# Norm powers by square root, reciprocal and a Newton step in lots; a planner that books the port of POOL and DVE; earlier first weight loads

## The chip, the cores and the metric

The kernel runs on one core of one Trainium2 chip. The metric is the device time of one execution in microseconds (us); the kernel before has a median of 950.0 us in 3 runs (944.38 to 951.93). The engines are TensorE (PE in the profile, its weight loads PEld), VectorE (DVE), ScalarE (ACT), GpSimd (POOL) and SyncE (SP), which issues every DMA here.

## The reference, cut to what matters

Three stages follow each other, all in float32. Attention without a softmax: B=4 batches, H=8 heads, S=576 rows, D=64:

```
kv  = einsum('bhsd,bhse->bhde', k, v)
out = einsum('bhsd,bhde->bhse', q, kv)
x   = out / sqrt(mean(out*out, -1) + 1e-6) * g_norm      # (4,8,576,64)
x   = x.transpose(0,2,1,3).reshape(2304, 512)
x   = (x @ w_a) * (x @ w_b) @ w_out                      # first MoE, d_ff 1536
x   = sigmoid(x @ w_gate) * (x @ w_val) @ w_out2         # second MoE
```

## The kernel before

**Attention.** The 2304 tokens are 18 tiles of 128 (`NTILE`). For each batch b, `keys_values` loads four blocks of keys and values (640 KB each), PE multiplies them into bank `o1` (L388) and ACT and DVE copy the result into `kvbd` (L399, L402). For each tile t, `queries` loads q (256 KB), PE multiplies (`O`, L422), ACT squares (L431), DVE sums the squares of each head (`ss`, L435), POOL scales (L439) and takes the power -0.5 of 128x8 elements (`rr`, L441), DVE multiplies PSUM by it (`xn`, L445), PE transposes (`T`, L452) and ACT writes the tile of x into `part` (`Y`, L458). Tiles 0 to 11 hold their product in one of the banks `u0` to `u5`; tiles 12 to 17 hold theirs in `o0` or `o1`, which the down products use too.

**Weights.** Each of 24 blocks F of 128 columns has tiles a, b and o (512 KB each, 64-bit numbers). `weights` loads one into a ring of two `raw` buffers (L208). ACT (L217, L221), DVE (L225, L227, L231) and POOL (L237) round it to float32 by integer operations. `w_parts` forms sums of the quarters on DVE (L256, L257, L262, L263) and splits each part into a high half on ACT (L273) and a low half (L277).

**MoE.** A group is a stage m, a pair of blocks q and one of three token ranges j; there are 36, in the order m, q, j. Each matrix product takes seven products of quarters (`SLOTS`, `ORDER`), 6 matmuls of 128x384 each (L494), for two blocks u and v; eight down products of the group before stand between them (`down`, L586, evicted at L594, L596, L598). With q = 0, `x_comb` builds the seven inputs of a range: DVE sums (`xs`, L307), ACT high halves (L326), low halves (`xl`, L329), and a store; later groups load them again.

**Order.** Nothing is ordered by hand. Every piece of work is an `op` with an engine, a planned duration, its predecessors, the buffers that it takes, and a due time. `Plan.order` runs the dues back from the products (the first is due at 38,000 ns) and then runs an event simulation: whenever an engine is free it takes the ready op with the earliest due time for which the buffer rings have room. What the plan does in turn is the program order of each engine, the SP queue of DMAs included; on the chip each engine keeps to that order. Ops with the two engines `LO` (the low halves, L277, L329, L566) go to whichever of DVE and POOL takes them first; DVE, which the loop over engines reaches before POOL, is planned at 0.55 of POOL's duration.

Of the kernel before, what the change touches and what calls it, by code (L numbers as in the profile page):

```python
# [23 lines left out]
P = 128  # L24
# [3 lines left out]
N = 384  # L28
# [21 lines left out]
ANY_ORDER = ("o0", "o1")  # L50


class Plan:


# [1 line left out]
    def __init__(self):  # L57
        self.ops, self.by, self.n = [], {}, 0

    def op(self, name, eng, ns, fn, after=(), new=(), uses=(), due=None, lag=150):  # L60
        o = dict(name=name, eng=(eng,) if isinstance(eng, str) else eng, ns=ns, fn=fn, new=list(new),
                 uses=list(uses) + [b for _, b in new], due=due, lag=lag, succ=[], need=0, at=None)
        self.by[name] = o
        o["after"] = list(after)
        self.ops.append(o)

    def order(self):
# [26 lines left out]
        events = [(0, i, "ready", o) for i, o in enumerate(ops) if not o["need"]]  # L94
        heapq.heapify(events)
        count, done = len(ops), []

        def room(o):
            for tag, b in o["new"]:
# [7 lines left out]
        while events:  # L107
            t = events[0][0]
            while events and events[0][0] <= t:
                _, _, what, o = heapq.heappop(events)  # L110
                if what == "ready":
                    for e in o["eng"]:
                        ready[e].append(o)
                elif what == "done":
                    for b in o["uses"]:
                        users[b] -= 1
                elif what == "lag":
                    for s in o["succ"]:
                        s["need"] -= 1
                        if not s["need"]:  # L120
                            for e in s["eng"]:
                                ready[e].append(s)
            for e in free_at:
                if free_at[e] > t:
                    continue
                best = None
                for o in ready[e]:
                    if (best is None or o["due"] < best["due"]) and room(o):
                        best = o
                if best is None:  # L130
                    continue
                for x in best["eng"]:
                    ready[x].remove(best)
                for tag, b in best["new"]:
                    ring = rings[tag]
                    if len(ring) >= RINGS.get(tag, 1):
                        ring.pop(0)
                    ring.append(b)
                    nxt[tag] += 1
                ns = best["ns"] * (0.55 if len(best["eng"]) == 2 and e == "DVE" else 1)  # L140
                best["at"], best["on"] = t, e
                done.append(best)
                free_at[e] = t + ns
                for end, what in ((t + ns, "done"), (t + ns, "free"), (t + ns + best["lag"], "lag")):
                    count += 1
                    heapq.heappush(events, (end, count, what, best))
# [6 lines left out]
def attention_then_two_moes(  # L153
# [22 lines left out]

    ident = one.tile([P, P], F32, name="ident")
    gcol = one.tile([P, 1], F32, name="gcol")
    mhalf = one.tile([P, H], F32, name="mhalf")
    kvbd = [one.tile([P, KC, P], F32, name=f"kvbd{i}") for i in range(2)]  # L180

    part = [one.tile([P, 2, KC, N], F32, name=f"part{j}") for j in range(NJ)]
# [9 lines left out]
        return 160 + 1.04 * n  # L192

    def pool(n):
        return 230 + 2.2 * n

    def dma(kb):
        return 150 + kb * 1024 / 390

    LO = ("POOL", "DVE")  # L200


    def weights(F, which):
        k = (F, which)
# [34 lines left out]
            )  # L239

        raw, m, l, w = (("raw", k), ("mag", k), ("last", k), ("w32", k))
        op(("load", k), "SP", dma(512), load, new=[("raw", raw)], lag=2000)
        op(m, "ACT", 670, mag, [("load", k)], [("mag", m)], [raw])
        op(l, "ACT", 670, last, [("load", k)], [("last", l)], [raw])
        op(("clamp", k), "DVE", 900, clamp, [m], uses=[m])
        op(("sign", k), "DVE", 750, sign, [("clamp", k)], uses=[raw, m])
        op(w, "POOL", 1400, rounded, [("sign", k), l], [("w32", w)], [m, l])

    def w_parts(F):

# [11 lines left out]
            V.tensor_tensor(out=t[:, 0:256], in0=tl[b][:, 256:512], in1=t1[:, 0:256], op=ALU.subtract)  # L262
            V.tensor_tensor(out=t[:, 256:512], in0=tl[a][:, 256:512], in1=t[:, 0:256], op=ALU.subtract)  # L263

        op(t13, "DVE", 950, sums13, [a, b], [("tmp", t13)], [a, b])
        op(t24, "DVE", 950, sums24, [t13], [("tmp", t24)], [a, b, t13])

        def parts(i, src, cut, n):
            name = ("wo" if i == "o" else f"wp{i}", F)

            def hi():
                tl[name] = new_tile(name[0], [2, n], F32R)
                A.activation(out=tl[name][:, 0, :], in_=tl[src][:, cut], func=ACTF.Copy)  # L273

            def lo(eng):
                t = tl[name]
                eng.tensor_tensor(out=t[:, 1, :], in0=tl[src][:, cut], in1=t[:, 0, :], op=ALU.subtract)  # L277

            op((*name, "h"), "ACT", act(n), hi, [src], [(name[0], name)], [src])
            op((*name, "l"), LO, pool(n), lo, [(*name, "h")], (), [src, name])  # L280

        parts(0, a, slice(0, 512), 512)
        parts(1, t13, slice(0, 512), 512)
# [10 lines left out]
    def x_comb(g, i, ready):  # L294
# [16 lines left out]
        if i in "563":  # L311
            args = {"5": (x21, x22, ALU.add), "6": (None, x11, ALU.subtract), "3": (x12, None, ALU.subtract)}[i]
            prev = {"5": [], "6": [("xl", g, "5")], "3": [("xl", g, "6")]}[i]
            op(("xs", g, i), "DVE", 1100, total(chain, "s12", *args), after + prev,
               [("s12", chain)] if i == "5" else [], [] if i == "5" else [chain])
            after, uses = [("xs", g, i)], [chain]
        elif i == "7":
            op(("xs", g, i), "DVE", 1100, total(s3, "s3", x11, x21, ALU.subtract), after, [("s3", s3)])
            after, uses = [("xs", g, i)], [s3]

        def source():
# [11 lines left out]
            nc.sync.dma_start(out=d, in_=tl[xin].rearrange("p a c n -> p (a c n)").bitcast(F32))  # L333

        op(("xh", g, i), "ACT", act(n), hi, after, [("xr", xin)], uses)
        op(("xl", g, i), LO, pool(n), lo, [("xh", g, i)], (), [xin, *uses])
        op(("xd", g, i), "SP", dma(768), store, [("xl", g, i)], (), [xin], lag=2000)
        return [("xl", g, i)]

# [26 lines left out]
    def keys_values(b):  # L366
# [38 lines left out]
        op(("V", b, 0), "ACT", 400, up, before, uses=[bank])  # L405
        op(("V", b, 1), "DVE", 430, dn, before, uses=[bank])

    def queries(t):
        q = ("q", t)
        bank, tbank = ("O", t), ("T", t)  # L410
# [18 lines left out]
        def square():  # L429
            tl["sq", t] = new_tile("sq", [H, D])  # L430
            A.activation(out=tl["sq", t], in_=heads(tl[bank]), func=ACTF.Square)  # L431

        def mean():
            tl["ss", t] = new_tile("ss", [H])
            V.tensor_reduce(out=tl["ss", t], in_=tl["sq", t], axis=mybir.AxisListType.X, op=ALU.add)  # L435

        def power():
            ss = tl["ss", t]
            G.tensor_scalar(out=ss, in0=ss, scalar1=1.0 / D, scalar2=EPS, op0=ALU.mult, op1=ALU.add)  # L439
            tl["rr", t] = new_tile("rr", [H, 1])  # L440
            G.tensor_tensor(out=tl["rr", t][:, :, 0], in0=ss, in1=mhalf, op=ALU.pow)  # L441

        def norm():
            tl["xn", t] = new_tile("xn", [KC, P])
            V.tensor_tensor(  # L445
                out=heads(tl["xn", t]), in0=heads(tl[bank]), in1=tl["rr", t].to_broadcast([P, H, D]), op=ALU.mult
            )

        def transpose():
# [7 lines left out]
        def to_x():  # L457
            A.activation(out=part[j][:, h, :, c:c + P], in_=tl[tbank], func=ACTF.Copy, scale=gcol[:, 0:1])  # L458

        sq, xn, ss, rr = (("sq", t), ("xn", t), ("ss", t), ("rr", t))  # L460
        op(q, "SP", dma(256), load, (), [("q", q)], lag=2000)
        op(bank, "PE", 1000, mm, [q] + [("V", i, e) for i, _, _ in batches(t) for e in (0, 1)]
           + ([('T', t - 2)] if t >= 12 + 2 else []), [(tag, bank)], [q])
        op(sq, "ACT", 610, square, [bank], [("sq", sq)], [bank])
        op(ss, "DVE", 720, mean, [sq], [("ss", ss)], [sq])
        op(rr, "POOL", 1950, power, [ss], [("rr", rr)], [ss])
        op(xn, "DVE", 720, norm, [rr], [("xn", xn)], [bank, rr])
        op(tbank, "PE", 480, transpose, [xn], [(ttag, tbank)], [xn])
        op(("Y", t), "ACT", 700, to_x, [tbank, "gcol"] + ([("K", in_part[t][0] + 1, in_part[t][1])] if t > 5 else []),
# [83 lines left out]
    def gated(g, uv, t, bank, other, after, due):  # L553
        me = ("P", g, uv)
        name = ("g", g, uv, t)

        def product_of():
            tl[me, "gf", t] = new_tile("gf", [N])
            V.tensor_tensor(out=tl[me, "gf", t], in0=tl[bank][:, :N], in1=tl[me, other], op=ALU.mult)  # L559

        def hi():
            tl[name] = new_tile(f"g{uv}{t}", [2, N], F32R)
            A.activation(out=tl[name][:, 0, :], in_=tl[me, "gf", t], func=ACTF.Copy)  # L563

        def lo(eng):
            eng.tensor_tensor(out=tl[name][:, 1, :], in0=tl[me, "gf", t], in1=tl[name][:, 0, :], op=ALU.subtract)  # L566

        gf = (me, "gf", t)
        op((*name, "f"), "DVE", dve(N), product_of, after, [("gf", gf)], [bank, (me, other)], due + 2800)
        op((*name, "h"), "ACT", act(N), hi, [(*name, "f")], [(f"g{uv}{t}", name)], [gf])  # L570
        op((*name, "l"), LO, pool(N), lo, [(*name, "h")], (), [gf, name])

    def down(g, k, due):
        m, q, j = g
# [85 lines left out]
    with tc.manual_schedule():  # L660
        warm = one.tile([P, 1], F32, name="warm")
        G.memset(warm, 0.0)
        A.activation(out=warm, in_=warm, func=ACTF.Square)
        make_identity(nc, ident)
        G.memset(mhalf, -0.5)
        V.memset(kvbd[1], 0.0)
        G.memset(kvbd[0], 0.0)
        for o in done:
# [35 lines left out]
```

## Time and profile before

| | |
|---|---|
| median of 3 runs | 950.0 us (944.38 to 951.93) |
| profiled execution, its own time | 950.53 us |
| its span, first to last instruction | 948.7 us |
| mean granted TensorE clock | 0.984 |
| busy PE, DVE, ACT, POOL | 901.6, 685.0, 416.3, 361.0 us |

The span is what the trace covers; 1.8 us of the execution lie outside it. Busy times are sums over all instructions of an engine, and an instruction that waits for a port in the middle counts as busy. A row of the timeline merges neighbouring instructions of one line.

### The profile page before, as it was taken

How to read it: one execution, taken by the hardware profiler on the slowest of the kernel's cores; microseconds unless marked ns; L12 is line 12 of the kernel's file. 1: busy time of each engine (PE TensorE's matmuls, PEld its weight loads, DVE VectorE, ACT ScalarE, POOL GpSimd, SP SyncE). 2: the span in 40 equal slices, each digit the busy share in tenths (PEclk: the TensorE clock that was granted, in tenths of full speed). 3: DMA queues.
4: the chain of work that ended last, by engine and by line, in shares of the span. 5: the costliest groups of instructions: out<-in, count | busy, mean ns of one | idle time of the engine just before them, and what ended most of it. 6: DMA issues, size and time to landing. Idle time of an engine off the chain costs nothing.

```text
span 948.7 us, 14074 instructions
## 1 busy us (share of the span) xinstructions
PE 901.6 (95%) x5144; PEld 888.1 (94%) x5144; DVE 685.0 (72%) x1135; ACT 416.3 (44%) x805; POOL 361.0 (38%) x289
## 2 busy tenths in 40 slices
PE   6698799999999999999998889999999999999998
PEld 6597689899999999999998889999999999999998
DVE  1899886688766767766779898678668668644445
ACT  2476553345333343333445556544444444333331
POOL 1787663444423423423447664223223323311101
PEclk9899989999999999999998999999999999999999
DMA  8975638988887787787775659787787787677783
GB/s 332 338 282 223 232 143 300 346 304 307 312 308 276 267 319 266 274 311 270 276 277 209 244 199 307 264 314 278 258 325 264 259 302 269 236 236 242 244 292 118
DMA packets 55222, 256.79 MB, mean 271 GB/s; under 512 B 6256, under 2 KB 9328, under 8 KB 55152
## 3 DMA queue, kind: packets, MB, share of 16 engines
q1 hardware_dynamic: 55152, 255.88, 75.2%
q8 instruction: 41, 0.67, 0.3%
q14 instruction: 29, 0.24, 0.1%
HBM read 218.10 MB, written 37.75 MB: 270 GB/s over the span
## 4 chain that ended last, share of the span: by engine, by line
PE 73%; DVE 12%; POOL 5%; DMA 4%; issue 4%; ACT 1%; SPq 0%; POOLq 0%; ACTq 0%; DVEq 0%
PE ps_u L494 45%; PE ps_o L586 27%; DMA raw<-w_all_dram 3%; POOL rr L441 2%; DVE s L307 2%; DVE xr L329 1%; DMA xr<-kv_in_dram 1%; DVE mag L225 1%; DVE mag L231 1%; POOL w L237 1%; POOL xr L329 1%; PE ps_o L388 1%; DVE tmp L256 1%; DVE gf L559 1%; DVE part L594 1%
## 5 line engine op out<-in xcount | busy, mean ns | idle before, releaser
L494 PE MATMUL ps_u<-xr,wp 128*128 128x384 f32 x3024 | 561.9, 339 | 7.6 <-POOL xr L329 2.6
L494 PEld LDWEIGHTS ps_u<-xr,wp 128*128 128x128 f32 x3024 | 534.1, 188 | 11.5 <-POOL xr L329 3.2
L586 PE MATMUL ps_o<-gu,wo 128*128 128x384 f32 x864 | 202.0, 342 | 19.2 <-DVE part L594 7.4
L586 PE MATMUL ps_o<-gv,wo 128*128 128x384 f32 x864 | 199.3, 338 | 0.0
L566 POOL TENSOR_TENSOR gu<-gf,gu 128x384 fp32r<-128x384 f32 x55 | 60.3, 1097 | 325.5 <-ACT gu L563 251.6
L594 DVE TENSOR_TENSOR part<-ps_o,part 128x384 f32<-128x384 f32 x240 | 131.6, 553 | 70.8 <-PE ps_o L586 70.4
L586 PEld LDWEIGHTS ps_o<-gu,wo 128*128 128x128 f32 x864 | 155.4, 191 | 25.3 <-DVE part L594 9.3
L586 PEld LDWEIGHTS ps_o<-gv,wo 128*128 128x128 f32 x864 | 156.9, 191 | 0.0
L237 POOL TENSOR_TENSOR w<-mag,last 128x512 int32<-128x512 int32 x72 | 102.4, 1429 | 69.0 <-DVE mag L231 54.9
L563 ACT ACTIVATE gu<-gf 128x384 fp32r<-128x384 f32 x72 | 37.6, 522 | 93.6 <-DVE gf L559 93.6
L217 ACT ACTIVATE mag<-raw 128x512 f32<-128x512 f32 x72 | 47.8, 666 | 61.3 <-DMA raw<-w_all_dram 40.5
L277 POOL TENSOR_TENSOR wp<-tmp,wp 128x512 fp32r<-128x512 f32 x23 | 31.7, 1380 | 88.1 <-ACT wp L273 87.9
L225 DVE TENSOR_SCALAR mag<-mag 128x512 f32<-128x512 f32 x72 | 40.6, 563 | 29.2 <-ACT mag L217 29.2
L273 ACT ACTIVATE wp<-tmp 128x512 fp32r<-128x512 f32 x48 | 29.7, 627 | 60.2 <-PE ps_u L494 40.1
L231 DVE SCALAR_TENSOR_TENSOR mag<-raw,mag 128x512 uint32<-128x512 uint32 x72 | 54.4, 756 | 0.8
L277 POOL TENSOR_TENSOR wp<-w,wp 128x256 fp32r<-128x256 f32 (+1 forms) x32 | 35.4, 1112 | 36.2 <-ACT wp L273 36.2
L221 ACT ACTIVATE last<-raw 128x512 int32<-128x512 uint32 x72 | 47.6, 662 | 0.0
L227 DVE TENSOR_SCALAR mag<-mag 128x512 uint32<-128x512 uint32 x72 | 44.1, 612 | 2.5
L563 ACT ACTIVATE gv<-gf 128x384 fp32r<-128x384 f32 x72 | 37.6, 522 | 16.2 <-DVE gf L559 15.3
L566 DVE TENSOR_TENSOR gv<-gf,gv 128x384 fp32r<-128x384 f32 x44 | 35.2, 800 | 10.1 <-ACT gv L563 8.9
L273 ACT ACTIVATE wp<-w 128x512 fp32r<-128x512 f32 (+1 forms) x48 | 24.4, 518 | 37.8 <-PE ps_u L494 30.9
L512 ACT ACTIVATE u2u<-ps_u 128x384 f32<-128x384 f32 x36 | 17.5, 486 | 52.7 <-PE ps_u L494 52.7
(73 smaller groups left out, 886.2 us busy)
## 6 DMA issues: line engine op xcount, KB each, us to landing
xr<-x SPq DMA_DIRECT2D x210, 768.0 KB, 5.6
raw<-w_all_dram SPq DMA_DIRECT2D x72, 512.0 KB, 5.9
x<-xr SPq DMA_DIRECT2D x42, 768.0 KB, 3.8
xr<-kv_in_dram SPq DMA_DIRECT2D x12, 640.0 KB, 6.1
q<-q_t_dram SPq DMA_DIRECT2D x18, 256.0 KB, 3.8
out_dram<-part SPq DMA_DIRECT2D x24, 192.0 KB, 2.1
part<-kv_in_dram SPq DMA_DIRECT2D x4, 640.0 KB, 7.0
gcol<-g_col_dram SPq DMA_DIRECT2D x1, 0.5 KB, 3.7
```

The source lines that it names most:

```text
L217: A.activation(out=tl["mag", k], in_=words(1).bitcast(F32), func=ACTF.Abs, scale=65536.0)
L221: A.activation(out=tl["last", k], in_=words(0), func=ACTF.Copy, scale=2.0**-29)
L225: V.tensor_scalar(out=m, in0=m, scalar1=LEAST, scalar2=MOST, op0=ALU.max, op1=ALU.min)
L231: V.scalar_tensor_tensor(out=m, in0=words(1), scalar=0x80000000, in1=m, op0=ALU.bitwise_and, op1=ALU.bitwise_or)
L237: G.tensor_tensor(out=tl["w32", k].bitcast(I32), in0=tl["mag", k].bitcast(I32), in1=tl["last", k], op=ALU.add)
L273: A.activation(out=tl[name][:, 0, :], in_=tl[src][:, cut], func=ACTF.Copy)
L277: eng.tensor_tensor(out=t[:, 1, :], in0=tl[src][:, cut], in1=t[:, 0, :], op=ALU.subtract)
L494: nc.tensor.matmul(out=o, lhsT=wt[:, a, c], rhs=x[:, b, k, :], start=(i in "152" and k == 0 and (a, b) == (0, 0)), stop=(k == 1 and (a, b) ...
L563: A.activation(out=tl[name][:, 0, :], in_=tl[me, "gf", t], func=ACTF.Copy)
L566: eng.tensor_tensor(out=tl[name][:, 1, :], in0=tl[me, "gf", t], in1=tl[name][:, 0, :], op=ALU.subtract)
L586: nc.tensor.matmul(out=o[:, :N], lhsT=tl["wo", f_of(g, uv)][:, a, c], rhs=tl["g", g, uv, t][:, b, :], start=(uv, a, b) == mms[0], stop=(uv ...
L594: V.tensor_tensor(out=acc, in0=o, in1=acc, op=ALU.add)
```

## The change

Five things change. The power of each tile is replaced by a chain for a lot of two or three tiles (`powers`): POOL scales, ACT takes the square root, DVE the reciprocal, and POOL makes one Newton step of five small operations; sums of squares of a lot share one tile. ACT's warming instruction becomes a Sqrt. The planner gets a flag `port` for DVE ops with operands in SBUF alone, and never plans such an op beside an op of POOL; POOL chooses before DVE and gives way to a more urgent op of DVE. The sums of `w_parts`, the `xs` sums and all low halves get the flag, as `clamp` and `sign` do in the diff. Planned durations are smaller (weights, sums, POOL). The loads of the first four weight tiles and of q for tiles 0 to 2 get due times. Product tiles 12 and 13 wait for the transposes of tiles 10 and 11 too.

```diff
+LOTS = [(0, 1, 2), (3, 4, 5), (6, 7, 8), (9, 10, 11), (12, 13), (14, 15), (16, 17)]
...
-            for e in free_at:
+            def first(e, port):
+                fit = [o for o in ready[e] if (port or e != "POOL" and not o["port"]) and room(o)]
+                return min(fit, key=lambda o: o["due"], default=None)
+
+            for e in ("PE", "ACT", "SP", "POOL", "DVE"):
                 if free_at[e] > t:
                     continue
-                best = None
-                for o in ready[e]:
-                    if (best is None or o["due"] < best["due"]) and room(o):
-                        best = o
+                best = first(e, e not in ("POOL", "DVE") or port_at <= t)
+                if e == "POOL" and best is not None and free_at["DVE"] <= t:
+                    other = first("DVE", True)
+                    if other is not None and other["port"] and (
+                        other["due"] < best["due"] or other is best and first("DVE", False) is None
+                    ):
+                        best = None
...
+                if e == "POOL" or e == "DVE" and best["port"]:
+                    port_at = t + ns
...
     def pool(n):
-        return 230 + 2.2 * n
+        return 200 + 2.12 * n
...
+    W_DUE = {(0, "a"): 17e3, (0, "b"): 17e3, (1, "a"): 20e3, (1, "b"): 20e3}
...
-        op(("load", k), "SP", dma(512), load, new=[("raw", raw)], lag=2000)
+        op(("load", k), "SP", dma(512), load, new=[("raw", raw)], due=W_DUE.get(k), lag=2000)
...
-        op(("clamp", k), "DVE", 900, clamp, [m], uses=[m])
-        op(("sign", k), "DVE", 750, sign, [("clamp", k)], uses=[raw, m])
-        op(w, "POOL", 1400, rounded, [("sign", k), l], [("w32", w)], [m, l])
+        op(("clamp", k), "DVE", 850, clamp, [m], uses=[m], port=True)
+        op(("sign", k), "DVE", 690, sign, [("clamp", k)], uses=[raw, m], port=True)
+        op(w, "POOL", 1300, rounded, [("sign", k), l], [("w32", w)], [m, l])
...
+    def powers(lot):
...
+            G.tensor_scalar(out=m, in0=m, scalar1=1.0 / D, scalar2=EPS, op0=ALU.mult, op1=ALU.add)
...
+            A.activation(out=tl["root", lot], in_=flat(tl[ss][:, :n, :]), func=ACTF.Sqrt)
...
+            V.reciprocal(out=tl["root", lot], in_=tl["root", lot])
...
+            G.tensor_scalar(out=m, in0=m, scalar1=3e38, scalar2=-0.5, op0=ALU.min, op1=ALU.mult)
+            G.tensor_tensor(out=m, in0=m, in1=y, op=ALU.mult)
+            G.tensor_tensor(out=m, in0=m, in1=y, op=ALU.mult)
+            G.tensor_scalar(out=m, in0=m, scalar1=1.5, scalar2=None, op0=ALU.add)
+            G.tensor_tensor(out=r, in0=m, in1=y, op=ALU.mult)
...
+        op(("ms", lot), "POOL", 280, mean_square, [("ss", t) for t in lot], uses=[ss])
+        op(root_, "ACT", 220, root, [("ms", lot)], [("root", root_)], [ss])
+        op(inv, "DVE", 200, inverse, [root_], uses=[root_])
+        op(rr, "POOL", 1500, newton, [inv], [("rr", rr)], [ss, root_])
...
-        def power():
-            ss = tl["ss", t]
-            G.tensor_scalar(out=ss, in0=ss, scalar1=1.0 / D, scalar2=EPS, op0=ALU.mult, op1=ALU.add)
-            tl["rr", t] = new_tile("rr", [H, 1])
-            G.tensor_tensor(out=tl["rr", t][:, :, 0], in0=ss, in1=mhalf, op=ALU.pow)
...
-        op(q, "SP", dma(256), load, (), [("q", q)], lag=2000)
+        op(q, "SP", dma(256), load, (), [("q", q)], due=18e3 if t < 3 else None, lag=2000)
...
-           + ([('T', t - 2)] if t >= 12 + 2 else []), [(tag, bank)], [q])
+           + ([('T', t - 2)] if t >= 12 else []), [(tag, bank)], [q])
...
+        first = t == lot[0]
+        op(("ss", t), "DVE", 720, mean, [sq] if first else [sq, ("ss", lot[0])], [("ss", ss)] if first else [],
+           [sq] if first else [sq, ss])
+        if t == lot[-1]:
+            powers(lot)
...
-        A.activation(out=warm, in_=warm, func=ACTF.Square)
+        A.activation(out=warm, in_=warm, func=ACTF.Sqrt)
```

## Rows read from the trace of the kernel before

**Rows 1.** Windows: each engine's busy us (instructions), granted clock, DMA share, GB/s.

```profile
0.00:20.00 20.00, 14.02 (x95) 13.64 (x96) 1.34 (x3) 2.79 (x5) 1.23 (x9) 1.00 0.90 353
20.00:60.00 40.00, 29.77 (x215) 27.93 (x215) 33.34 (x48) 23.94 (x43) 32.20 (x28) 0.87 0.79 285
60.00:120.00 60.00, 48.71 (x288) 44.12 (x286) 54.00 (x80) 36.19 (x65) 43.91 (x36) 0.97 0.66 249
120.00:150.00 30.00, 26.66 (x132) 24.88 (x133) 27.26 (x33) 16.72 (x30) 17.77 (x12) 0.89 0.54 198
...
200.00:500.00 300.00, 300.00 (x1712) 299.62 (x1711) 222.36 (x401) 120.86 (x237) 107.17 (x87) 1.00 0.81 291
500.00:600.00 100.00, 91.39 (x488) 89.06 (x488) 88.59 (x118) 56.63 (x107) 55.57 (x34) 0.95 0.66 244
```

**Rows 2.** Chain of waits to 120 us: start, us, what.

```profile
20.78 0.08 issue
...
29.16 6.08 DMA raw<-w_all_dram
...
36.04 0.44 DVE mag L225
...
47.57 0.68 DVE ss L435
```

**Rows 3.** Timeline of PE: start, us, line, instructions, idle before and its cause.

```profile
17.14 1.38 PE L388 MATMUL ps_o<-xr 128*128 128x128 f32 x10 [0.28 <-DMA xr<-kv_in_dram]
22.48 3.32 PE L422 MATMUL ps_u<-kvbd,q 128*128 128x128 f32 x32 [1.28 <-DMA q<-q_t_dram]
45.71 1.09 PE L452 MATMUL ps_o<-ident,xn 128*128 128x128 f32 x4 [5.35 <-DVE kvbd L402]
56.49 1.30 PE L494 MATMUL ps_u<-xr,wp 128*128 128x384 f32 x6
```

**Rows 4.** Timeline of SP's DMA issues to 42 us: start, us, line.

```profile
0.72 10.77 SPq L380 DMA_DIRECT2D xr<-kv_in_dram  x8
...
12.97 0.97 SPq L208 DMA_DIRECT2D raw<-w_all_dram  x2
29.16 2.33 SPq L208 DMA_DIRECT2D raw<-w_all_dram  x2
```

**Rows 5.** Groups to 125 us: line, count, busy us, mean ns, idle before.

```profile
L441 POOL TENSOR_TENSOR rr<-ss,mhalf 128x8 f32<-128x8 f32 x18 | 31.7, 1760 | 1.5
L439 POOL TENSOR_SCALAR ss<-ss 128x8 f32<-128x8 f32 x18 | 5.8, 325 | 22.7 <-DVE ss L435 21.4
L663 ACT ACTIVATE warm<-warm 128x1 f32<-128x1 f32 x1 | 0.2, 203 | 0.0
```

**Rows 6.** Timeline of POOL and DVE: POOL's power, DVE beside it; POOL's rounding, DVE beside it.

```profile
21.14 1.88 POOL L441 TENSOR_TENSOR rr<-ss,mhalf 128x8 f32<-128x8 f32 x1
22.55 0.43 DVE L227 TENSOR_SCALAR mag<-mag 128x512 uint32<-128x512 uint32 x1
...
39.37 1.38 POOL L237 TENSOR_TENSOR w<-mag,last 128x512 int32<-128x512 int32 x1 [0.63 <-DVE mag L231]
39.66 1.37 DVE L227 TENSOR_SCALAR mag<-mag 128x512 uint32<-128x512 uint32 x1
```

**Rows 7.** Waits of PE, 60 to 200 us: total us, times, longest.

```profile
PE ps_o L586 <- DVE xn L445: 7.0, 5, 2.4
PE ps_u L494 <- POOL xr L329: 2.6, 2, 1.5
```

**Rows 8.** Groups of ACT over the whole span: table loads.

```profile
L663 ACT ACT_TABLE_LOAD x1 | 1.3, 1283 | 0.7 <-PEq L693 0.7
L530 ACT ACT_TABLE_LOAD x1 | 1.3, 1283 | 0.0
```

**Rows 9.** The page's groups: the low halves of the gated product.

```profile
L566 POOL TENSOR_TENSOR gu<-gf,gu 128x384 fp32r<-128x384 f32 x55 | 60.3, 1097 | 325.5 <-ACT gu L563 251.6
...
L566 DVE TENSOR_TENSOR gv<-gf,gv 128x384 fp32r<-128x384 f32 x44 | 35.2, 800 | 10.1 <-ACT gv L563 8.9
```

More of the change, by code (lines that the diff above doesn't have):

```diff
@@ L58, in __init__, with op @@
         self.ops, self.by, self.n = [], {}, 0
-    def op(self, name, eng, ns, fn, after=(), new=(), uses=(), due=None, lag=150):
+    def op(self, name, eng, ns, fn, after=(), new=(), uses=(), due=None, lag=150, port=False):
         o = dict(name=name, eng=(eng,) if isinstance(eng, str) else eng, ns=ns, fn=fn, new=list(new),
-                 uses=list(uses) + [b for _, b in new], due=due, lag=lag, succ=[], need=0, at=None)
+                 uses=list(uses) + [b for _, b in new], due=due, lag=lag, port=port, succ=[], need=0, at=None)
         self.by[name] = o
@@ L96, in order @@
         count, done = len(ops), []
+        port_at = 0
         def room(o):
@@ L178, in attention_then_two_moes @@
     gcol = one.tile([P, 1], F32, name="gcol")
-    mhalf = one.tile([P, H], F32, name="mhalf")
     kvbd = [one.tile([P, KC, P], F32, name=f"kvbd{i}") for i in range(2)]
@@ L263, in sums24 @@
             V.tensor_tensor(out=t[:, 256:512], in0=tl[a][:, 256:512], in1=t[:, 0:256], op=ALU.subtract)
-        op(t13, "DVE", 950, sums13, [a, b], [("tmp", t13)], [a, b])
-        op(t24, "DVE", 950, sums24, [t13], [("tmp", t24)], [a, b, t13])
+        op(t13, "DVE", 840, sums13, [a, b], [("tmp", t13)], [a, b], port=True)
+        op(t24, "DVE", 840, sums24, [t13], [("tmp", t24)], [a, b, t13], port=True)
         def parts(i, src, cut, n):
@@ L279, in parts @@
             op((*name, "h"), "ACT", act(n), hi, [src], [(name[0], name)], [src])
-            op((*name, "l"), LO, pool(n), lo, [(*name, "h")], (), [src, name])
+            op((*name, "l"), LO, pool(n), lo, [(*name, "h")], (), [src, name], port=True)
         parts(0, a, slice(0, 512), 512)
@@ L313, in x_comb @@
             prev = {"5": [], "6": [("xl", g, "5")], "3": [("xl", g, "6")]}[i]
-            op(("xs", g, i), "DVE", 1100, total(chain, "s12", *args), after + prev,
-               [("s12", chain)] if i == "5" else [], [] if i == "5" else [chain])
+            op(("xs", g, i), "DVE", 960, total(chain, "s12", *args), after + prev,
+               [("s12", chain)] if i == "5" else [], [] if i == "5" else [chain], port=True)
             after, uses = [("xs", g, i)], [chain]
         elif i == "7":
-            op(("xs", g, i), "DVE", 1100, total(s3, "s3", x11, x21, ALU.subtract), after, [("s3", s3)])
+            op(("xs", g, i), "DVE", 960, total(s3, "s3", x11, x21, ALU.subtract), after, [("s3", s3)], port=True)
             after, uses = [("xs", g, i)], [s3]
@@ L335, in x_comb @@
         op(("xh", g, i), "ACT", act(n), hi, after, [("xr", xin)], uses)
-        op(("xl", g, i), LO, pool(n), lo, [("xh", g, i)], (), [xin, *uses])
+        op(("xl", g, i), LO, pool(n), lo, [("xh", g, i)], (), [xin, *uses], port=True)
         op(("xd", g, i), "SP", dma(768), store, [("xl", g, i)], (), [xin], lag=2000)
@@ L406, in keys_values, with flat, mean_square, root @@
         op(("V", b, 1), "DVE", 430, dn, before, uses=[bank])
+    def powers(lot):
+        n = len(lot)
+        ss, rr = ("ss", lot), ("rr", lot)
+        def flat(t):
+            return t.rearrange("p a h -> p (a h)")
+        def mean_square():
+            m = flat(tl[ss][:, :n, :])
+            G.tensor_scalar(out=m, in0=m, scalar1=1.0 / D, scalar2=EPS, op0=ALU.mult, op1=ALU.add)
+        def root():
+            tl["root", lot] = new_tile("root", [3 * H])[:, :n * H]
+            A.activation(out=tl["root", lot], in_=flat(tl[ss][:, :n, :]), func=ACTF.Sqrt)
+        def inverse():
+            V.reciprocal(out=tl["root", lot], in_=tl["root", lot])
+        def newton():
+            m, y = flat(tl[ss][:, :n, :]), tl["root", lot]
+            tl[rr] = new_tile("rr", [3, H, 1])
+            r = tl[rr][:, :n].rearrange("p a h o -> p (a h o)")
+            G.tensor_scalar(out=m, in0=m, scalar1=3e38, scalar2=-0.5, op0=ALU.min, op1=ALU.mult)
[3 more added lines that the diff above has]
+            G.tensor_tensor(out=r, in0=m, in1=y, op=ALU.mult)
+        root_, inv = ("root", lot), ("inv", lot)
+        op(("ms", lot), "POOL", 280, mean_square, [("ss", t) for t in lot], uses=[ss])
+        op(root_, "ACT", 220, root, [("ms", lot)], [("root", root_)], [ss])
+        op(inv, "DVE", 200, inverse, [root_], uses=[root_])
+        op(rr, "POOL", 1500, newton, [inv], [("rr", rr)], [ss, root_])
     def queries(t):
@@ L431, in square @@
             A.activation(out=tl["sq", t], in_=heads(tl[bank]), func=ACTF.Square)
+        lot = next(x for x in LOTS if t in x)
         def mean():
-            tl["ss", t] = new_tile("ss", [H])
-            V.tensor_reduce(out=tl["ss", t], in_=tl["sq", t], axis=mybir.AxisListType.X, op=ALU.add)
-        def power():
-            ss = tl["ss", t]
-            G.tensor_scalar(out=ss, in0=ss, scalar1=1.0 / D, scalar2=EPS, op0=ALU.mult, op1=ALU.add)
-            tl["rr", t] = new_tile("rr", [H, 1])
-            G.tensor_tensor(out=tl["rr", t][:, :, 0], in0=ss, in1=mhalf, op=ALU.pow)
+            if t == lot[0]:
+                tl["ss", lot] = new_tile("ss", [3, H])
+            V.tensor_reduce(
+                out=tl["ss", lot][:, t - lot[0], :], in_=tl["sq", t], axis=mybir.AxisListType.X, op=ALU.add
+            )
         def norm():
@@ L445, in norm @@
             V.tensor_tensor(
-                out=heads(tl["xn", t]), in0=heads(tl[bank]), in1=tl["rr", t].to_broadcast([P, H, D]), op=ALU.mult
+                out=heads(tl["xn", t]), in0=heads(tl[bank]), in1=tl["rr", lot][:, t - lot[0]].to_broadcast([P, H, D]), op=ALU.mult
             )
@@ L458, in to_x @@
             A.activation(out=part[j][:, h, :, c:c + P], in_=tl[tbank], func=ACTF.Copy, scale=gcol[:, 0:1])
-        sq, xn, ss, rr = (("sq", t), ("xn", t), ("ss", t), ("rr", t))
-        op(q, "SP", dma(256), load, (), [("q", q)], lag=2000)
+        sq, xn, ss, rr = (("sq", t), ("xn", t), ("ss", lot), ("rr", lot))
+        op(q, "SP", dma(256), load, (), [("q", q)], due=18e3 if t < 3 else None, lag=2000)
         op(bank, "PE", 1000, mm, [q] + [("V", i, e) for i, _, _ in batches(t) for e in (0, 1)]
-           + ([('T', t - 2)] if t >= 12 + 2 else []), [(tag, bank)], [q])
+           + ([('T', t - 2)] if t >= 12 else []), [(tag, bank)], [q])
         op(sq, "ACT", 610, square, [bank], [("sq", sq)], [bank])
-        op(ss, "DVE", 720, mean, [sq], [("ss", ss)], [sq])
-        op(rr, "POOL", 1950, power, [ss], [("rr", rr)], [ss])
+        first = t == lot[0]
[3 more added lines that the diff above has]
+            powers(lot)
         op(xn, "DVE", 720, norm, [rr], [("xn", xn)], [bank, rr])
@@ L570, in gated @@
         op((*name, "h"), "ACT", act(N), hi, [(*name, "f")], [(f"g{uv}{t}", name)], [gf])
-        op((*name, "l"), LO, pool(N), lo, [(*name, "h")], (), [gf, name])
+        op((*name, "l"), LO, pool(N), lo, [(*name, "h")], (), [gf, name], port=True)
     def down(g, k, due):
@@ L662, in attention_then_two_moes @@
         G.memset(warm, 0.0)
-        A.activation(out=warm, in_=warm, func=ACTF.Square)
+        A.activation(out=warm, in_=warm, func=ACTF.Sqrt)
         make_identity(nc, ident)
-        G.memset(mhalf, -0.5)
         V.memset(kvbd[1], 0.0)
```

## The prediction

> **What bounds the kernel now.** I first read the windows by stage [rows 1]. From 200 to 500 us TensorE is busy all the time: nothing there can be won, only lost. It is idle for 6.0 us of the first 20, 10.2 of the next 40, 11.3 from 60 to 120, 3.3 from 120 to 150, and 8.6 from 500 to 600, where the second MoE begins. In the same stretches the granted clock falls to 0.87, 0.97, 0.89 and 0.95: part of the work there runs at 1.2 instead of 2.4 GHz. DVE is at 83%, 90% and 91% of the three stretches from 20 to 150 us, against 74% in the full one. So the beginning is held by DVE and by what DVE waits for, and the end of the program moves with the moment at which TensorE's stream gets going.
>
> The chain of waits says which work that is [rows 2]: from 29.16 to 47.57 us it runs through the second pair of weight tiles, the last 11.5 us of it on DVE. The timeline of TensorE shows the price [rows 3]: the transpose of tile 4 starts at 45.71, behind 5.35 us of idle time, the first MoE product only at 56.49. The planner had that product due at 38 us. SP's timeline shows why the weights come in the middle [rows 4]: eight key loads go first, the first two weight tiles are issued at 12.97, and the next two at 29.16, when the ring of two buffers is free again. Until 20 us DVE is busy for 1.34 us and ACT for 2.79 [rows 1].
>
> **Part one: the early weight loads.** By hand from the code, the due times put (0,a) and (0,b), and the three q loads, among or ahead of the first keys, which are due at about 17 to 22 us; (1,a) and (1,b), due at 20, follow when `raw` has room. Four weight tiles (2.0 MB) and three q loads (0.75 MB) thus move past up to eight key loads on SP. At the 353 GB/s of the first window, 2.9 MB (with binary units) take 8.2 us. The last keys of batch 1 are multiplied until 18.52 [rows 3], so they end by about 26.7 at the worst. SP keeps its order: where the load of (1,a) waits for DVE to finish the sign of (0,a), every key load behind it waits too. Cover for that are the transfers already issued; if it is gone, the wait is inside the 8.2 us again, not on top of it, as long as the weights are through by then.
>
> What is gained: DVE's block from 36.04 to 47.57 (11.5 us, with one copy of 0.43 that stays: 11.1) goes into the idle time before 20 us. What is lost: tiles 0 to 3 need batch 0 alone, whose squares were taken at 19.45 because q stood behind the keys; they start about then again. Tiles 4 and 5 need batch 1. Their products ran inside the row that starts at 22.48 and ends at 25.80, after a wait for q; with keys until 26.7 they come about 2 us later. Net 11.1 - 2 = 9.1, and I add 0.9 for the two signs of the first pair, which then leave the norm's queue on DVE too: **10 us**. Ends: nothing, if later stages give it all back, and 18.4 us, the whole stretch of rows 2.
>
> **Part two: the powers.** Out go 18 powers of 1.760 us and 18 scalings of 0.325, 37.5 us of POOL [rows 5]. In come 7 lots of six small POOL operations. The nearest row below is the scaling (0.325, 8 elements a partition), the nearest above the rounding (1.38, 512 elements) [rows 6]; 24 elements are near 8, so 0.33: 7 x 6 x 0.33 = 13.9 us. POOL is rid of 23.6 us (at 1.38 it would pay 20.5 us instead). ACT gets 7 roots; the one-element ACTIVATE took 0.203 [rows 5], and ACT is idle for 23.8 of 60 us [rows 1], so no cost but latency. DVE gets 7 reciprocals, at most the 0.43 of a 512-element operation [rows 6]: 3 us at the worst, about 1.4 likely. A lot's chain, 6 x 0.33 + 0.2 + 0.2 and about eight hand-overs of 0.08 [rows 2], is 3.0 us where a single tile's took 0.33 + 1.76 + 0.16 = 2.2; three tiles in turn took 6.7.
>
> Does a power also hold DVE up? In rows 6 a shift on DVE beside a power (21.14 to 23.02) takes 0.43 us; the same instruction beside a rounding of full width takes 1.37 and ends just after it. So a power hardly holds the port, and its removal gives POOL time but DVE little. The Trainium skill (SBUF — State Buffer, section SBUF: two separate sides) says that the instruction that starts first has the shared pair for its whole length; the long row agrees, the power's row does not. By that rule the removal would also free the port for the 31.7 us of the powers; that is a rival below.
>
> TensorE waits 7.0 us for `xn` and 2.6 for low halves of x between 60 and 200 us [rows 7], 9.6 together. The last three lots hold both output banks while their chain runs, and down products queue behind them. I take **2.5 us**; ends: 3 lost (the longer chain once for each of the last three lots) and 9.6 won.
>
> **Part three: the planner.** It changes the order on every engine, not the work. Where the port is crowded, 500 to 600 us, a truer plan may win a part of the 8.6 us of idle time and of the half clock; or lose as much. I take **1 us**, ends 8.6 either way. From 200 to 500 us I cost it at nothing: DVE has 77.6 and POOL 193 us of idle time there, which hides the order. The bank edge for tiles 12 and 13, the memset and the warming Sqrt are nothing.
>
> **Sum.** 10 + 2.5 + 1 = 13.5 us off the profiled execution's own 950.5 (span 948.7, 1.8 outside): 937.0. That execution lies 0.5 above the median of 950.0.
>
> **The rivals.**
> 1. *Given back.* TensorE starts early, but DVE, at 90% from 60 to 150 us, cannot feed groups 0 to 2 faster; of the ten only some 3 remain. 950.5 - 3 - 2.5 = 945. For it: the 90%. Against: part of those 90% is waiting for the port, and POOL, with 23.6 us less, can take low halves from DVE.
> 2. *Keys late.* Weights and q hold the keys back by the full 8.2 us and the first product follows them: 11.1 - 8.2 = 3 won, 2.5 of the powers: again 945.
> 3. *The steady stage pays.* POOL now chooses first and plans no operation beside DVE's; a low half costs 1.097 on POOL, 0.800 on DVE [rows 9]. If the gated product's low halves arrive later than the down products that need them, TensorE waits in each of the 36 groups. From 13.5 / 36 = 0.38 us a group the change is a loss; at 1 us it ends at 950.5 - 13.5 + 36 = 973. Against it: full occupancy with much slack beside it.
> 4. *Table loads.* Two are there now: before the first ACTIVATE, and before the first Sigmoid, after which Abs and Copy go on without another [rows 8]. If Square did not share Sqrt's table, each lot would load twice: 14 x 1.283 = 18 us of ACT, with some 2.6 us more in each chain; about half of seven on the path gives 937 + 9 = 946. The Trainium skill (ScalarE: Activation LUTs, section Table sets: the hidden batching unit) tells to batch by set and counts a switch dearer than the row; it lists the cheap functions as members of all sets, without a word on Square there.
> 5. *More than forecast.* Norm, weights and the port all ease: first product near 38, as planned (18 us), 5 us of rows 7 and 4 of the transition: 950.5 - 27 = 924. The rule of the whole-length hold leads here.
>
> **How the numbers follow.** A measurement of this kernel tells about 1% (9.5 us) from no change. The forecast has 0.42, the fifth rival 0.18: 0.60 for faster by over 1%. Rivals 1, 2 and 4 have 0.15, 0.08 and 0.06: 0.29 within 1%. The third has 0.11. The likeliest time is 937. The range takes in most of the fifth rival at 924, and 1, 2 and 4 with some room to 951; outside are the third and the far end of the fifth. The forecast's own range is 929 to 941.
>
> **What would show it.** Weight tiles rounded before 20 us; the first MoE product between 42 and 48 us; the key products of batch 1 ended by 27; POOL's norm work near 14 us and POOL's low halves more; DVE's waits for a root or a Newton step small; two table loads; TensorE still without idle time from 200 to 500 us. A first product before 48 with TensorE's idle time after it grown by as much would show the first rival; idle time in the steady stage the third.

## The result, and the profile after

The changed kernel takes 925.85 us (median; 924.51 to 927.02) against 950.49 before: ratio 0.9752, 95% interval 0.9707 to 0.9797, some 24 us less. The time lies within the range, but the likeliest value, 937, was 11 us too high, and most of the gain does not come from where the prediction put it.

The windows of after, cut as in [rows 1] (busy us and instructions of PE, PEld, DVE, ACT, POOL; clock, DMA share, GB/s):

```profile
0.00:20.00 20.00, 9.12 (x43) 8.44 (x44) 12.36 (x23) 9.39 (x16) 5.37 (x11) 0.96 0.92 364
20.00:60.00 40.00, 33.95 (x260) 31.63 (x258) 23.41 (x39) 20.15 (x38) 14.23 (x29) 0.93 0.84 301
60.00:120.00 60.00, 47.93 (x291) 44.89 (x291) 47.58 (x77) 37.52 (x69) 32.08 (x39) 0.95 0.63 235
120.00:150.00 30.00, 29.63 (x158) 28.67 (x158) 23.64 (x37) 18.32 (x33) 14.40 (x11) 0.93 0.67 243
...
200.00:500.00 300.00, 298.36 (x1704) 297.71 (x1703) 209.59 (x385) 121.70 (x235) 113.20 (x94) 1.00 0.80 287
500.00:600.00 100.00, 100.00 (x574) 100.00 (x573) 83.98 (x135) 62.95 (x119) 50.15 (x35) 1.00 0.76 280
```

From 60 to 120 us TensorE is idle for 12.1 us, before for 11.3: nothing is won there. From 500 to 600 us it has no idle time and the full clock, and issues 574 instructions instead of 488; at the full stage's pace (1712 in 300 us before, 0.175 us each) the 86 are 15 us: the 8.6 us of idle time that before had there, and the rest half clock. That is most of the gain. Progress shows it better than idle time. Matmuls of the MoE (products and downs), counted in windows of each trace:

| kernel | to 120 us | 120 to 200 | 500 to 600 | ratio to before, interval |
|---|---|---|---|---|
| before | 210 | 393 | 488 | |
| after | 207 | 436 | 574 | 0.9752 (0.9707 to 0.9797) |
| planner alone (e1) | 201 | 425 | 572 | 0.9792 (0.9760 to 0.9823) |
| early loads alone (e2) | 220 | 404 | 490 | 0.9926 (0.9898 to 0.9954) |
| lots alone (e3) | 182 | 360 | 489 | 1.0051 (1.0027 to 1.0074) |
| planner and lots (e4) | 192 | 406 | 576 | 0.9780 (0.9751 to 0.9809) |
| planner and loads (e9) | 222 | 445 | 578 | 0.9655 (0.9627 to 0.9683) |
| new durations and order, no port (e7) | 240 | 409 | 463 | 0.9970 (0.9951 to 0.9989) |
| port booked, nothing else (e8) | 222 | 384 | 572 | 0.9811 (0.9781 to 0.9842) |

At 120 us the changed kernel is no further than the one before. It is level there, wins 7.5 us (43 matmuls) to 200 us and 15 in the transition to the second MoE, from 500 to 600.

What happens in the transition is best seen in a stretch where TensorE stood for 3.1 us before. A port operation is here one of DVE with its operands in SBUF alone, as flagged in the plan. Timeline of before, 509 to 517 us (start, us, engine, line, instruction, idle before):

```profile
509.18 4.28 POOL L329 TENSOR_TENSOR xr<-part,xr 128x768 fp32r<-128x768 f32 x2
509.55 2.20 DVE L566 TENSOR_TENSOR gv<-gf,gv 128x384 fp32r<-128x384 f32 x1
...
511.68 2.60 DVE L307 TENSOR_TENSOR s<-part 128x768 f32<-128x768 f32 x1
...
516.00 0.54 DVE L594 TENSOR_TENSOR part<-ps_o,part 128x384 f32<-128x384 f32 x1
...
516.60 0.69 PE L586 MATMUL ps_o<-gu,wo 128*128 128x384 f32 x1 [3.10 <-DVE part L594]
```

Two low halves of x occupy POOL from 509.18 to 513.46. The low half of v on DVE, next to them, takes 2.20 us where its fastest took 0.546, and the sum behind it 2.60 instead of 0.943. The eviction that TensorE needs (it reads PSUM) stands behind both, and behind three short instructions, in DVE's queue until 516.00. The same stretch after:

```profile
509.40 1.84 POOL L346 TENSOR_TENSOR xr<-s,xr 128x768 fp32r<-128x768 f32 x1 [2.31 <-ACT xr L343]
...
510.20 0.56 DVE L649 TENSOR_TENSOR part<-ps_o,part 128x384 f32<-128x384 f32 x1 [0.48 <-PE ps_o L641]
510.68 0.85 DVE L242 TENSOR_SCALAR mag<-mag 128x512 f32<-128x512 f32 x1
...
513.28 1.85 POOL L346 TENSOR_TENSOR xr<-part,xr 128x768 fp32r<-128x768 f32 x1 [2.03 <-ACT xr L343]
513.37 0.56 DVE L649 TENSOR_TENSOR part<-ps_o,part 128x384 f32<-128x384 f32 x1 [0.92 <-PE ps_o L641]
```

While POOL works, DVE evicts PSUM at 0.56 us each, so such an eviction would have run beside POOL before too; only the tail of POOL's first operation still meets a port operation (0.85 instead of 0.43). The page's busy line adds it up:

```profile
PE 890.8 (96%) x5144; PEld 882.6 (95%) x5144; DVE 638.0 (69%) x1129; ACT 423.4 (46%) x812; POOL 334.5 (36%) x307
```

DVE is busy for 47 us less than before (685.0) with six instructions fewer: 13 low halves have gone to POOL, seven reciprocals have come. At the shortest times of their lines these are some 6 us less work, so by this estimate some 41 us were time spent waiting for the port in the middle of an instruction. (A busy time counts the moments in which two instructions of an engine overlap once; it is not the sum of their durations.)

### The profile page after: what moved, and what is told of

It is laid out like the page before. It is cut to its first block, busy times and chain, and to the rows that moved or that the text cites. A ratio compares the mean times of both kernels' runs of the same rounds, so it can differ in the third digit from the quotient of the medians.

```text
span 925.2 us, 14091 instructions
## 1 busy us (share of the span) xinstructions
PE 890.8 (96%) x5144; PEld 882.6 (95%) x5144; DVE 638.0 (69%) x1129; ACT 423.4 (46%) x812; POOL 334.5 (36%) x307
## 4 chain that ended last, share of the span: by engine, by line
PE 87%; DMA 5%; DVE 3%; POOL 1%; issue 1%; ACT 1%; SPq 0%; POOLq 0%; ACTq 0%
PE ps_u L549 54%; PE ps_o L641 32%; DMA raw<-w_all_dram 4%; DMA xr<-kv_in_dram 1%; PE ps_u L475 1%; PE ps_o L405 1%; DVE s L324 1%; DVE xn L497 1%; DMA x<-xr 0%; PE ps_o L504 0%; DVE mag L244 0%; POOL xr L346 0%; ACT xr L343 0%; DVE xr L346 0%; ACT mag L234 0%
## 5 line engine op out<-in xcount | busy, mean ns | idle before, releaser
L549 PE MATMUL ps_u<-xr,wp 128*128 128x384 f32 x3024 | 554.3, 336 | 2.7 <-ACT xr L343 1.1
L621 POOL TENSOR_TENSOR gu<-gf,gu 128x384 fp32r<-128x384 f32 x53 | 56.3, 1062 | 273.4 <-ACT gu L618 223.3
L254 POOL TENSOR_TENSOR w<-mag,last 128x512 int32<-128x512 int32 x72 | 97.7, 1362 | 109.3 <-DVE mag L248 106.0
L294 POOL TENSOR_TENSOR wp<-tmp,wp 128x512 fp32r<-128x512 f32 x28 | 37.5, 1344 | 96.5 <-ACT wp L290 96.1
L242 DVE TENSOR_SCALAR mag<-mag 128x512 f32<-128x512 f32 x72 | 35.2, 489 | 36.5 <-ACT mag L234 36.5
L248 DVE SCALAR_TENSOR_TENSOR mag<-raw,mag 128x512 uint32<-128x512 uint32 x72 | 49.9, 695 | 0.8
L294 POOL TENSOR_TENSOR wp<-w,wp 128x256 fp32r<-128x256 f32 (+1 forms) x30 | 30.0, 1001 | 39.8 <-ACT wp L290 39.7
L618 ACT ACTIVATE gv<-gf 128x384 fp32r<-128x384 f32 x72 | 37.6, 522 | 14.2 <-DVE gf L614 13.9
L346 POOL TENSOR_TENSOR xr<-s,xr 128x768 fp32r<-128x768 f32 x16 | 31.1, 1945 | 33.3 <-ACT xr L343 30.7
L244 DVE TENSOR_SCALAR mag<-mag 128x512 uint32<-128x512 uint32 x72 | 40.7, 566 | 2.5
```

Of the source, the lines that this page charges most:

```text
L244: V.tensor_scalar(out=m, in0=m, scalar1=3, scalar2=None, op0=ALU.logical_shift_left)
L248: V.scalar_tensor_tensor(out=m, in0=words(1), scalar=0x80000000, in1=m, op0=ALU.bitwise_and, op1=ALU.bitwise_or)
L254: G.tensor_tensor(out=tl["w32", k].bitcast(I32), in0=tl["mag", k].bitcast(I32), in1=tl["last", k], op=ALU.add)
L549: nc.tensor.matmul(out=o, lhsT=wt[:, a, c], rhs=x[:, b, k, :], start=(i in "152" and k == 0 and (a, b) == (0, 0)), stop=(k == 1 and (a, b) ...
```

## The experiments

**The parts alone.** After the result stood a second account, the planner theory: the new order makes the gain, the loads and the lots next to nothing. The first four runs set it against the prediction's sum (loads 10, powers 2.5, planner 1).

e1, the new planner without `powers` and without the due times (the code of before in both places), with the edge

```diff
-           + ([('T', t - 2)] if t >= 12 + 2 else []), [(tag, bank)], [q])
+           + ([('T', t - 2)] if t >= 12 else []), [(tag, bank)], [q])
```

> The kernel before with the new planner alone (port flag, POOL first, new durations, and the edge that makes tile products 12 and 13 wait for transposes 10 and 11, without which the new plan finds no end); powers per tile and late weight loads as before. Planner theory: 926 to 936 us, TensorE's idle time from 500 to 600 us (8.6) near 0. The prediction's sum: 1 us off, 949.

930.33 us. The planner alone brings 20 of the 24 us.

e2, the due times alone:

```diff
-        op(("load", k), "SP", dma(512), load, new=[("raw", raw)], lag=2000)
+        op(("load", k), "SP", dma(512), load, new=[("raw", raw)], due=W_DUE.get(k), lag=2000)
-        op(q, "SP", dma(256), load, (), [("q", q)], lag=2000)
+        op(q, "SP", dma(256), load, (), [("q", q)], due=18e3 if t < 3 else None, lag=2000)
```

> The kernel before with the due times of the first four weight loads and of q for tiles 0 to 2 alone. Planner theory: the first product comes some us earlier and TensorE is no further at 120 us: 946 to 954 us. The prediction's sum: 10 us off, 940.

944.31 us, 7 us off (4 to 10 by the interval): between the two, nearer to the prediction. TensorE was 10 matmuls further at 120 us, so the planner theory was too hard on the loads.

e3, the lots alone (`powers`, Sqrt as the warming function, and the edge for tiles 12 and 13; the rest of the planner, durations and loads of before):

> The kernel before with the powers by lots alone, the old planner and the late loads. Planner theory: POOL is rid of some 24 us, and TensorE gains 0 to 4 us: 946 to 952. The prediction's sum: 2.5 us off, 948. If the powers did hold the port over their whole length: 940 or less.

955.92 us, slower by 0.27% to 0.74%. Neither theory had that. What the edge has of it was not measured; e7 below has the edge too and is not slower.

e4, after without the due times (the diff of e2 undone):

> The changed kernel without the due times of the weight and q loads. Planner theory: the early loads are worth nothing or cost, as keys of batches 1 and 2 come late behind them: 922 to 930 us. The prediction's sum: 10 us lost, 936.

929.76 us: at the end of the planner theory's range. Beside planner and lots the loads are worth some 3 us, by intervals that overlap.

**What in the planner does it.** e5, after with the port ignored:

```diff
-                 uses=list(uses) + [b for _, b in new], due=due, lag=lag, port=port, succ=[], need=0, at=None)
+                 uses=list(uses) + [b for _, b in new], due=due, lag=lag, port=False, succ=[], need=0, at=None)
-                if e == "POOL" or e == "DVE" and best["port"]:
+                if False:
```

> The changed kernel with a planner that ignores the port (flag off, nothing booked; POOL still first, the new durations, lots and early loads stay). If booking the port is what the planner's 20 us come from: 942 to 952 us, and from 500 to 600 us TensorE waits for evictions by DVE again (8 us or more). If the new durations and the order of engines do it: 923 to 932.

966.02 us, ratio 1.0181 (1.0152 to 1.0210): worse than expected of either; from 500 to 600 us TensorE waits 11.7 us for DVE's evictions again. Without the booking, the rest of the change is a loss. e7 makes the same cut in e1:

> The kernel before with the new durations, POOL first and the bank edge, but no port booked; powers and loads as before. If the booking alone makes the planner's gain: no gain, 948 to 968 us, waits of TensorE for evictions by DVE from 500 to 600 as before. If durations and order do it: 926 to 936.

948.06 us, at the edge of the expectation: durations, order and edge without the booking win 0.1% to 0.5%. e8 adds to the kernel before nothing but flag, booking and bank edge:

```diff
+                    if (e == "POOL" or o["port"]) and port_at > t and e in ("POOL", "DVE"):
+                        continue
                     if (best is None or o["due"] < best["due"]) and room(o):
...
+                if e == "POOL" or e == "DVE" and best["port"]:
+                    port_at = t + ns
```

> The kernel before with the booking of the port alone (flag and bank edge; DVE still first, old durations, no giving way). If the booking alone makes the gain: 928 to 938 us, TensorE without idle time from 500 to 600. If it needs the rule by which POOL gives way and the tighter durations: 942 to 952.

932.92 us. The booking alone is worth 18 us (15 to 21); the interval of the whole planner (e1) overlaps this one. The busy lines of e7 and of e8:

```profile
PE 899.7 (95%) x5144; PEld 886.8 (94%) x5144; DVE 656.6 (69%) x1105; ACT 419.2 (44%) x805; POOL 397.4 (42%) x319
```

```profile
PE 891.2 (96%) x5144; PEld 881.6 (95%) x5144; DVE 633.2 (68%) x1131; ACT 420.6 (45%) x805; POOL 344.2 (37%) x293
```

DVE and POOL together: 1046 us before, 1054 in e7, 977 in e8, with the same powers in all three. From 500 to 600 us TensorE waits in e7 as it did before, and for longer; e8 has no wait at all there. Up to 200 us e8 is where before was (606 and 603 matmuls), so the booking's gain lies in the transition, and the 40 more that the changed kernel has by 200 us come from the rest of the change. Timeline of TensorE in e7, 500 to 600 us, its instructions after a wait:

```profile
512.52 1.33 PE L603 MATMUL ps_o<-gu,wo 128*128 128x384 f32 x3 [4.96 <-DVE part L611]
541.61 1.33 PE L603 MATMUL ps_o<-gu,wo 128*128 128x384 f32 x3 [3.61 <-DVE part L615]
570.78 0.79 PE L603 MATMUL ps_o<-gu,wo 128*128 128x384 f32 x3 [2.96 <-DVE part L615]
```

**Why the lots cost.** TensorE's waits in after, total us, times, longest:

```profile
PE ps_o L405 <- DMA xr<-kv_in_dram: 10.2, 5, 4.7
PE ps_o L641 <- DVE xn L497: 9.4, 3, 4.7
PE ps_u L475 <- DMA q<-q_t_dram: 2.0, 1, 2.0
```

The wait for `xn` grew from 7.0 [rows 7] to 9.4. The longest of the three, in the timeline: the second sum of squares of a pair, its chain, and the down product that waits for the bank.

```profile
113.13 0.67 DVE L491 TENSOR_REDUCE ss<-sq 128x8 f32<-128x512 f32 x1
...
113.55 1.29 POOL L294 TENSOR_TENSOR wp<-tmp,wp 128x512 fp32r<-128x512 f32 x1
...
114.92 0.53 POOL L436 TENSOR_SCALAR ss<-ss 128x16 f32<-128x16 f32 x1
115.48 0.22 ACT L440 ACTIVATE root<-ss 128x16 f32<-128x16 f32 x1 [0.51 <-POOL ss L436]
115.53 1.26 POOL L254 TENSOR_TENSOR w<-mag,last 128x512 int32<-128x512 int32 x1
115.73 0.25 DVE L443 RECIPROCAL root<-root 128x16 f32<-128x16 f32 x1 [0.34 <-ACT root L440]
...
116.88 0.28 POOL L449 TENSOR_SCALAR ss<-ss 128x16 f32<-128x16 f32 x1
...
118.19 0.22 POOL L453 TENSOR_TENSOR rr<-ss,root 128x16 f32<-128x16 f32 x1
...
118.44 1.29 DVE L497 TENSOR_TENSOR xn<-ps_o,rr 128x512 f32<-128x512 f32 x2 [2.46 <-POOL rr L453]
119.19 1.33 PE L641 MATMUL ps_o<-gu,wo 128*128 128x384 f32 x3 [4.74 <-DVE xn L497]
```

From the start of the sum at 113.13 to the end of the Newton step at 118.41 are 5.3 us, 4.6 of them behind the sum; the small operations take 2.2 (0.53 + 0.22 + 0.25, and five from 0.22 to 0.28). A low half of a weight (1.29 us) stands ahead of the first one on POOL, the one planned at 0.28 us, and a rounding of 1.26 us between the root and the Newton step. A chain that crosses engines five times meets their queues five times, and the pair holds both output banks for as long.

e6, tiles 12 to 17 one by one:

```diff
-LOTS = [(0, 1, 2), (3, 4, 5), (6, 7, 8), (9, 10, 11), (12, 13), (14, 15), (16, 17)]
+LOTS = [(0, 1, 2), (3, 4, 5), (6, 7, 8), (9, 10, 11), (12,), (13,), (14,), (15,), (16,), (17,)]
```

> The changed kernel with tiles 12 to 17 as lots of one. If pairs that hold both output banks cause TensorE's waits for xn (9.4 us in three waits at 87, 103 and 119 us): those fall below 6 us and the time to 920 to 924. If the waits come from DVE's and POOL's queues whatever the lot: 924 to 929, waits as before.

922.74 us; the wait for `xn` no longer appears among TensorE's waits of 0.8 us and more. So the pairs cause it. The time is 3 us lower, by intervals that overlap (0.9717, 0.9694 to 0.9740); i2 below settles that single lots gain.

e9, after with a power per tile again (e1 with the due times):

> The changed kernel with a power per tile again (new planner, early loads). If the lots earn what the prediction gave them beside the new planner: 928 to 930 us, 2.5 above the changed kernel. If the powers cost nothing once the port is planned: 922 to 927. If a plan that takes each power for 1.95 us of the port is poor: 932 or more.

918.27 us, ratio 0.9655 (0.9627 to 0.9683) against 0.9752 (0.9707 to 0.9797) with the lots. Below all three expectations: with the port planned and the loads early, the single power is better than the lots by 8 to 9 us (7.6 by the medians, 9.2 by the ratios), though POOL is busy for 368.0 us instead of 334.5. It is also better than e6, where the last six tiles have their chains one by one, so the pairs are not all of it; whether the rest is the chain itself or the lots of three was not tried. And it changes what the loads are worth: with a power per tile they bring some 12 us beside the planner (e1 930.33, e9 918.27; intervals apart), with the lots some 3.

**Why the first product came late.** In after it starts at 53.17, before at 56.49 [rows 3], forecast was 42 to 48. TensorE's timeline, and SP's, suggest why:

```profile
39.17 1.38 PE L405 MATMUL ps_o<-xr 128*128 128x128 f32 x10 [0.23 <-DMA xr<-kv_in_dram]
...
41.48 0.65 PE L504 MATMUL ps_o<-ident,xn 128*128 128x128 f32 x4
...
53.17 2.35 PE L549 MATMUL ps_u<-xr,wp 128*128 128x384 f32 x12
```

```profile
11.19 4.55 SPq L397 DMA_DIRECT2D xr<-kv_in_dram  x5
23.50 3.28 SPq L468 DMA_DIRECT2D q<-q_t_dram  x2
26.83 1.45 SPq L397 DMA_DIRECT2D part<-kv_in_dram  x1
```

The scaled tile 0 was there at 34.1, but its transpose stands behind the keys of batch 2 in TensorE's order, and these were issued only from 26.83 on: SP stood from 15.74 to 23.50 for one of three q buffers.

i1, six buffers for q:

```diff
-         "gf": 2, "q": 3, "xn": 2, "ss": 2, "rr": 2}
+         "gf": 2, "q": 6, "xn": 2, "ss": 2, "rr": 2}
```

> The changed kernel with six buffers for q instead of three. If the SP queue, standing from 15.7 to 23.5 us for a q buffer, makes the keys of batch 2 and with them the first product late: no such stop, first product before 48 us, 917 to 923 us. If the stage to 120 us is bound by DVE and POOL: first product earlier, time 924 to 928.

926.12 us: SP no longer stops there (the q loads go out at 16.84), but the first product comes at 52.80 and the time is unchanged. The stop was not the limit: the keys of batch 2 end at 40.19 (40.55 in after) although they are issued earlier, and the transposes still stand behind them. i2, six buffers and single lots:

> Both: six q buffers and lots of one for tiles 12 to 17. If both causes hold and add: 913 to 920. If the early stage gives both back: 924 to 928.

918.24 us, 4.5 less than e6 and 7.9 less than i1: together the two give more than the sum of both alone. Beside i1 (0.9673, 0.9655 to 0.9690, against 0.9747, 0.9727 to 0.9768) the single lots are a clear gain. The first product moves from 55.23 in e6 to 50.31; why the buffers move it here and not beside the pairs stays open. i8, six buffers on top of e9:

> The new planner and the early loads with a power per tile, and six buffers for q. If the stop of SP for a q buffer is what still makes the first product late there: first product before 52 us, 912 to 916 us. If the queues of DVE and POOL bind by then, as with pairs: 917 to 920.

914.58 us, ratio 0.9615 (0.9571 to 0.9659): the fastest measured, below both kernels. Its interval overlaps that of e9, so the buffers' own share is not settled. The first product came at 50.42, in e9 at 50.67: the buffers do not bring it forward here. TensorE's longest wait there is its first, 10.3 us for the keys of batch 0, which stand behind weights and q on SP.

## Why the prediction was right, and where it was not

**The sum** had the right sign and a range that held, by errors that cancelled, which is luck: the parts it priced at 10, 2.5 and 1 us are worth 7, -5 and 20 alone. Nor do they simply add, as the sum takes for granted: the loads are worth 7, 12 or 3 us, by what stands beside them.

**Part three, the planner, failed.** The step was "I take 1 us, ends 8.6 either way". The end took the idle time of 500 to 600 us for all that could be won; the half clock that follows the stops (granted clock 0.79, 0.87 and 0.83 in before from 510 to 520, 520 to 530 and 540 to 550 us) was named but not added, and the 43 matmuls to 200 us were left out. Above all the value was chosen without a row. The rows were there: [rows 6] shows one instruction stretched from 0.43 to 1.37 us, and the lines of before show means far above their minima all over the transition (the sums of x: 1.92 us in four instructions, at least 0.94).

```profile
510.00:520.00 10.00, 6.89 (x31) 6.44 (x31) 9.93 (x12) 4.89 (x8) 5.37 (x4) 0.79 0.66 266
520.00:530.00 10.00, 10.00 (x52) 10.00 (x51) 6.51 (x11) 4.16 (x8) 1.89 (x2) 0.87 0.57 220
...
540.00:550.00 10.00, 7.12 (x32) 6.78 (x31) 9.96 (x11) 4.65 (x9) 7.17 (x5) 0.83 0.63 249
```

```profile
L307 DVE TENSOR_TENSOR s<-part 128x768 f32<-128x768 f32 x4 | 7.7, 1918 | 0.0
```

Summed over the span the changed kernel has some 41 us less of such waiting on DVE. The prediction used the row to price the powers and not the plan. What the plan is worth, the booking shows: 18 us alone (e8), and e5 and e7 lose it when only the booking goes.

**Part one** said 11.1 us of DVE's work would move into the idle start: it did (DVE 12.36 us busy before 20 us, 1.34 before). "Keys by 26.7 at the worst": they ended at 29.55.

```profile
19.26 2.50 PE L405 MATMUL ps_o<-xr 128*128 128x128 f32 x10 [1.22 <-DVE kvbd L419]
...
23.26 2.27 PE L405 MATMUL ps_o<-xr 128*128 128x128 f32 x10
...
28.27 1.28 PE L405 MATMUL ps_o<-xr 128*128 128x128 f32 x10
```

No late load held them: from 20 to 30 us TensorE was never idle, but the granted clock was 0.73, ten key products took 2.50 and 2.27 us where they took 1.28 later, three tile products stood between them, and the first waited for DVE's copy of `kvbd`, behind the early weights in DVE's queue. "First product between 42 and 48": 53.17. The forecast followed DVE's chain and forgot TensorE's own order, in which the transposes stand behind the next batch's keys. The loads alone gave 7 us, and 12 beside the planner with a power per tile, so the size of part one was fair; in the changed kernel about 3 are left, the size that the rival "given back" named. Its mark, a first product before 48, did not come, and its cause, DVE too full to feed the first groups, is not what the runs show: with the same planner and loads the powers (e9) keep the gain and the lots lose it.

**Part two** was right on the work: POOL's norm operations take 12.4 us (forecast 13.9), the reciprocals 1.9, two table loads remain, so Square runs without another load beside Sqrt:

```profile
L718 ACT ACT_TABLE_LOAD x1 | 1.3, 1283 | 0.7 <-PEq L747 0.7
L585 ACT ACT_TABLE_LOAD x1 | 1.3, 1283 | 0.0
```

It was wrong on the sign. The chain was priced at 3.0 us, undisturbed; in the pair above it took 4.6 behind the sum, and the queues were the difference. The lower end, 3 lost, was some 2 short of e3.

**The rule of the whole-length hold** (the Trainium skill, SBUF — State Buffer, section SBUF: two separate sides) would have freed 31.7 us of the port with the powers. Lots alone gave no gain (e3), which alone would not settle it, since the chains cost too. The rows do: of the port operations that start beside one of the 18 powers in before, 17 by the trace, none is over 0.02 us longer than the shortest of its line. A power of 8 elements does not keep DVE from the port. For full-width operations the rule and the stretch at 509 us agree.

**Rival three** did not come: 298.4 of 300 us busy in the full stage. **Rival five** had the right time, 924, by another sum.

Left open: why e7 is further at 120 us than all others of the table (240 matmuls); it loses that in the transition (463). A plan that books the port only behind the first stage was not tried.

## What to carry to other kernels

An instruction that runs two or three times its minimum may be a queue in disguise: compare means with minima for each line, and look at what stands behind the long ones in their engine's order. Where two engines share a resource, let the order know it; here one bound in the planner was worth 18 us, while 25 us less work on an engine off the path (POOL's norm, 37.5 to 12.4 us) were worth nothing. Before a short operation is split into a chain over several engines, count the queues it enters and the buffers it holds meanwhile.

## What the runs showed of the hardware

A power of -0.5 on 128x8 elements takes POOL 1.64 us at best and leaves DVE's port operations at their own 0.43 us. On 128x24 elements a root takes ACT 0.22 us, a reciprocal DVE 0.29, each step on POOL 0.21 to 0.30 at best. The expectation for the small steps, 0.33, held (0.30 on average); what was not expected is that a stretched DVE instruction costs TensorE time through the PSUM evictions queued behind it: 3.1 us of idle time at 513 us, and half clock after it.
